# A two-stage attention and token-mixing kernel on one core: all operations in a new order

## The chip, the cores and the metric

The kernel runs on one core of a Trainium2 chip. The core has five engines that run side by side, each with its own queue of instructions taken in order: TensorE (PE: matmuls, with their weight loads shown apart as PEld), VectorE (DVE), ScalarE (ACT), GpSimd (POOL) and SyncE (SP, which here only requests transfers). Transfers between memory (DRAM) and on-chip memory (SBUF) are requested by an instruction in some engine's queue and run on 16 DMA engines. Matmul results go to PSUM, eight banks of 512 float32 columns over 128 partitions, and are brought to SBUF by VectorE or ScalarE ("evicted"). The metric is the device time of one execution in microseconds.

## The reference

Batch 8, 8 heads, 576 tokens, head size 64, 32 packed queries, model size 512, hyper size 64. All inputs and the output are float32.

```python
def sm_attn(qq, kk, vv):                      # per batch and head
    s = scale * np.matmul(qq, kk.transpose(0, 1, 3, 2))
    s = s - np.max(s, axis=-1, keepdims=True)
    a = np.exp(s)
    a = a / (np.sum(a, axis=-1, keepdims=True) + 1e-09)
    return np.matmul(a, vv)
p_packed = sm_attn(p, k, v)                   # 32 rows per head
out = sm_attn(q, p_packed, p_packed)          # 576 rows per head
...
x = out.transpose(0, 2, 1, 3).reshape(B, S, H * D)
wq = x @ w_q
wk = x @ w_k
W_tok = scale * np.einsum('bsd,btd->bst', wq, wk)
mixed = np.einsum('bst,btd->bsd', W_tok, x)
return np.maximum(mixed, 0.0) @ w_out
```

## The kernel before

The work is cut into some 650 small operations. Each is a Python function that issues one to some tens of instructions, and a long string, SCHEDULE, names them one after another: `kt1@2:3` is operation kt1 for batch 2 with PSUM bank 3, `ke1@2s` its eviction on ScalarE (`s`; `v` is VectorE, `g` GpSimd), and a letter `f` or `c` says whether a matmul takes all 128 weight columns at once or two halves. The loop at lines 827 to 833 walks through the string and calls the functions. Every engine gets its instructions in the order of the string, and the waits between engines are put in by the framework. So the string alone sets each engine's queue.

The operations for one batch, in the order of the data:

- LK, LQ, LV (line 149): loads of k, q and v, requested by GpSimd, converted to bfloat16 on the way. Batch 0's k comes differently: KA and KB (line 170) load its two halves as float32 (k_f) from SyncE's queue, and cA0, cA1, cB0, cB1 (line 251) cast them. PF (line 167) requests p of batch 0 (p_f) from ScalarE's queue, pfc (line 215) casts it to p_h, tp (line 220) transposes it, lp (line 227) scales it into pT_bd. PB (line 180) loads p of all batches; tr and lq (lines 234 and 242) do the same for batches 1 to 7. cw0 to cw3 (line 279) load w_q and w_k (wqk), wo0 and wo1 (line 288) w_out.
- kt0, kt1 (line 305): transposes of k, evicted by ke0, ke1 to kT; for batch 0 kf0 to kf3 (line 258) and kfe0 to kfe3. qt0, qt1, qe0, qe1: the same for q.
- s0 (line 346): scores of the packed queries. nm0 (line 356): their row maximum. ex0, ex1 (line 360): exponentials with row sums. rc1 (line 370), rm (line 409, GpSimd): reciprocal and a mask with it. xt0, xt1 (line 377), xe0, xe1: transposes of the exponentials. pv (line 422): times v. pp (line 431): normalised and masked. pt, pte: transposed (ppT).
- e0, e1 (line 471), e2 (line 484): scores of the 576 queries against the packed rows. For batches 0 to 3 mn0 to mn2 (line 532) take the negative maximum, ea0 to ea2 (line 540) add it on TensorE, xa0 to xa2 (line 546) exponentiate; for batches 4 to 7 mx, sb and x0 (lines 501, 505 and 556) do so with a subtraction on VectorE.
- sm0 (line 562, or on GpSimd lines 565 to 568): row sums. rr0 (line 572): reciprocals. ml0 to ml2 (line 576): normalised weights a, products of two tensors on VectorE or GpSimd.
- at0, at1 (lines 596 and 599), ae0, ae1: transposes of a. pq (line 450), pqe: packed rows times w_q and w_k. wk, wz, wq (lines 654, 665 and 686), g (709), y (725), m0, m1 (740), r (the relu), m2 (765), then o0 to o4 (line 782): the mixing and the projection, and st0 to st2 and sc (lines 816, 812 and 800) the stores, requested by SyncE.
- w1, w2 (line 204): filler matmuls on zeros, whose results are not used.

Nearly all evictions run through one helper, `evict`, so many rows of the profile carry its lines: 136 (ScalarE), 138, 140 and 142 (VectorE).

Buffers rotate by batch: six each for k, q and v. Requests of GpSimd stand in its queue between its arithmetic.

Of the kernel before, what the change touches and what calls it, by code (L numbers as in the profile page):

```python
# [7 lines left out]


SCHEDULE = """  # L10
    id@0 PB@0 w1@0c:1 LQ@0 w1@0c:0 w1@0c:0 w1@0c:5 PF@0 LV@0 w1@0c:7 w1@0c:1 KB@0 LK@1 w2@0c:2
    pfc@0s LK@2 w1@0c:1 cB0@0v KA@0 LQ@1 cB1@0v w1@0c:2 cA1@0s w1@0f:3 kf2@0:7 kfe2@0v w1@0c:3 cw1@0
    kf3@0:1 cA0@0v tp@0:7 lp@0s w1@0f:6 kf0@0:0 kfe3@0v cw0@0 cw2@0 kfe0@0v kf1@0:3 kfe1@0s tr@0:76
    lq1@0s cw3@0 s0@0:3 qt0@0:2 w1@0f:0 w1@0f:0 nm0@0 ex0@0 ex1@0 w1@0f:6 lq0@0s qt1@0:0 xt0@0c:4
    xt1@0f:3 w1@0f:5 rc1@0 qe1@0v w1@0f:0 LV@1 rm@0 xe0@0v w1@0f:7 xe1@0s pv@0:3 qe0@0v w1@0c:0 pp@0
    pt@0c:2 pte@0v e0@0c:4 kt1@1:1 ke1@1s mn0@0 e2@0:3 mn2@0 kt0@1:0 ke0@1v e1@0c:7 w1@0f:5 mn1@0
    LK@3 LQ@2 ea2@0c LV@2 s0@1:0 ea0@0c LK@4 xa2@0 ea1@0f xa0@0 w1@0c:5 nm0@1 xa1@0 sm0@0v wo1@0
    ex0@1 kt1@2:3 wo0@0 rr0@0 ml0@0v ex1@1 w1@0f:5 kt0@2:7 ke1@2s ke0@2s qt1@1:5 ml1@0v qe1@1v
    xt0@1c:1 qt0@1:2 xt1@1c:0 LV@3 xe1@1v rc1@1 rm@1 ml2@0v at0@0f:4 qe0@1s w1@0f:3 s0@2:5 at1@0f:3
    pq@0:2 xe0@1v ae0@0s pv@1:0 nm0@2 ae1@0s pqe@0s ex0@2 wk@0f:2 wz@0 pp@1 pt@1c:0 pte@1v LQ@3  # L20
    wq@0:1 wkx@0 ex1@2 e1@1f:0 e0@1f:5 mn0@1 e2@1:7 mn2@1 wke@0s g@0f:2 ge@0v wqe@0s xt1@2f:4
    xt0@2f:6 ea0@1c mn1@1 xe1@2s kt1@3:2 xe0@2v LK@5 xa0@1 ea2@1f xa2@1 ea1@1f xa1@1 ke1@3v pq@1:6
    rc1@2 y@0:4 ye@0v pqe@1s kt0@3:1 ke0@3s rm@2 w1@0f:2 m1@0:45 sm0@1v rr0@1 ml1@1g r11@0s qt1@2:2
    qe1@2s qt0@2:1 qe0@2v s0@3:5 pv@2:1 r10@0s ml0@1g nm0@3 m0@0:04 pp@2 pt@2f:1 r00@0v ex1@3
    at0@1f:2 pte@2v ml2@1g ex0@3 r01@0v LQ@4 at1@1f:3 e1@2f:1 e0@2f:0 ae0@1s LV@4 mn1@2 ae1@1s LK@6
    e2@2:6 mn2@2 kt0@4:7 kt1@4:4 ke1@4s LQ@5 ke0@4v mn0@2 wk@1f:3 wz@1 wke@1v wkx@1 wq@1:2 ea2@2c
    rc1@3 rm@3 xa2@2 ea1@2c xa1@2 pq@2:7 pqe@2s wqe@1v ea0@2c xa0@2 s0@4:3 xt0@3f:6 xe0@3s xt1@3f:1
    xe1@3s nm0@4 g@1f:2 sm0@2v rr0@2 o3@0f:7 LK@7 ml1@2g ge@1s ml2@2v ex1@4 ex0@4 rc1@4 o2@0f:0
    ml0@2g o0@0c:2 oe0@0v LV@5 oe3@0s y@1:3 pv@3:5 LV@6 pp@3 ye@1s xt0@4f:1 xe0@4v m1@1:34 r11@1v
    rm@4 oe2@0s m0@1:27 r00@1v qt0@3:0 qt1@3:5 r10@1s xt1@4c:4 r01@1s xe1@4s pt@3c:7 pte@3v LQ@6  # L30
    at1@2f:2 m2@1f:1 qe1@3v at0@2f:7 qe0@3s o1@0f:4 ae0@2s e1@3f:3 e0@3f:6 r2@1v kt1@5:0 ae1@2v
    pq@3:5 mn1@3 mn0@3 e2@3:2 mn2@3 oe1@0s pqe@3v ea1@3c kt0@5:7 LQ@7 ea0@3f ea2@3f ke1@5s xa1@3
    ke0@5v xa0@3 wk@2f:4 wz@2 qt1@4:0 wq@2:3 wke@2v wkx@2 qe1@4v s0@5:5 g@2f:4 xa2@3 sm0@3g wqe@2s
    qt0@4:0 ge@2s y@2:3 ye@2s nm0@5 ex0@5 ex1@5 qe0@4v pv@4:1 pp@4 o2@1c:3 rr0@3 m0@2:01 oe2@1s
    m1@2:24 r11@2s ml0@3g pt@4f:5 r10@2s r01@2s pte@4v o1@1f:6 e1@4f:5 e0@4f:4 r00@2v at0@3f:0
    ae0@3s oe1@1v mx0@4 xt0@5f:2 e2@4:6 xe0@5s kt0@6:1 pq@4:3 pqe@4s ke0@6s mx2@4 o0@1c:0 ml1@3g
    kt1@6:2 oe0@1s mx1@4 ml2@3g sb2@4 st0@1 qt1@5:6 xt1@5f:1 at1@3f:0 sb1@4 sb0@4 x0@4 ae1@3s ke1@6v
    s0@6:3 rc1@5 qe1@5v sm0@4g o4@1f:2 xe1@5s wk@3f:0 kt0@7:1 nm0@6 ex1@6 kt1@7:6 wz@3 rm@5 oe4@1v
    ke0@7v wkx@3 ke1@7v qt0@5:2 wq@3:1 ex0@6 rc1@6 wke@3s qe0@5s pv@5:3 s0@7:5 rr0@4 pp@5 xt0@6f:2
    pt@5f:3 ml0@4g wqe@3s nm0@7 xt1@6f:4 g@3f:0 LV@7 o3@1f:1 pte@5s e0@5f:3 ge@3v xe0@6s ml1@4g  # L40
    o2@2f:2 e1@5f:0 ex0@7 xe1@6v ml2@4g at1@4f:4 mx0@5 ex1@7 at0@4f:5 sb0@5 oe3@1s y@3:6 mx1@5
    e2@5:3 rm@6 st1@0 oe2@2s ye@3s ae0@4s xt0@7c:1 rc1@7 rm@7 mx2@5 sb1@5 sb2@5 ae1@4v xe0@7s
    o3@2c:2 pv@6:6 pp@6 x0@5 m0@3:51 m1@3:03 r00@3s wk@4f:4 pt@6f:6 r01@3v wq@4:7 pte@6v oe3@2v
    pq@5:1 wz@4 st1@2 r10@3s pqe@5v wke@4v qt1@6:5 qt0@6:2 sm0@5g r11@3s o0@3c:0 qe0@6v o1@3c:1
    qe1@6s e0@6c:2 wkx@4 g@4c:3 e1@6c:5 wqe@4s oe1@3s st0@0 oe0@3v rr0@5 xt1@7c:6 mx0@6 e2@6:7
    qt1@7:0 xe1@7s ge@4v st1@1 st2@1 ml0@5g mx1@6 sb1@6 o0@2c:4 qe1@7s at0@5c:6 m2@3c:3 mx2@6 sb2@6
    o1@2c:5 ml1@5g sb0@6 ae0@5s ml2@5g at1@5c:0 r2@3s pv@7:1 x0@6 oe0@2s y@4:6 ae1@5v pp@7 ye@4v
    qt0@7:3 oe1@2s sm0@6g st0@3 wq@5:0 pt@7c:4 wk@5c:1 pte@7s m0@4:62 m1@4:75 qe0@7v wqe@5s wz@5
    wkx@5 wke@5v e0@7c:4 mx0@7 o4@3c:3 pq@7:0 r10@4s o2@3c:1 r00@4s sb0@7 r01@4s e2@7:2 e1@7c:7
    pq@6:6 rr0@6 mx1@7 r11@4s g@5c:4 mx2@7 sb2@7 pqe@7s oe4@3s o2@4c:0 ge@5s oe2@3s pqe@6s y@5:3  # L50
    ye@5s o3@3c:1 sb1@7 m2@5c:2 ml0@6g at0@6c:7 x0@7 ae0@6v ml1@6g r2@5s ml2@6g o3@4c:4 at1@6c:3
    oe2@4s sm0@7v ae1@6s o0@4c:5 st0@2 oe0@4s m1@5:07 rr0@7 ml2@7g ml1@7v m0@5:63 r00@5v ml0@7g
    o1@4c:2 r10@5s oe1@4v wk@6c:0 r01@5s at1@7c:6 wz@6 ae1@7v at0@7c:3 ae0@7v wq@6:5 o4@5c:2 st2@3
    wk@7c:3 wq@7:6 st0@4 r11@5s oe3@4s oe3@3s wqe@6s wz@7 o1@5c:5 wke@6s wqe@7s wkx@6 st1@3 g@6c:0
    oe1@5s ge@6s wkx@7 wke@7v g@7c:6 ge@7s o3@5c:3 st1@4 y@6:5 y@7:0 o2@5c:4 ye@6s oe3@5s m0@6:56
    r00@6s ye@7v m1@6:30 o0@5c:7 m2@7c:1 oe4@5v m0@7:52 r10@6v oe2@5v r11@6s st2@5 m1@7:03 r01@6s
    o0@6c:6 o1@6c:4 r00@7v r10@7v o2@6c:5 oe0@5s st0@5 oe0@6s r11@7v o3@6c:0 st1@5 oe1@6s r2@7v
# [12 lines left out]
def kernel(  # L70
# [460 lines left out]
    def nmax2(i, b):  # L531
        nc.vector.tensor_reduce(
            units(i, tile("mn", [P, NU, 1], bf16, b)), S_[b]["e", i], axis=AX, op=MAX, negate=True)

# [329 lines left out]
```

## Time and profile before

| what | value |
|---|---|
| median of 3 runs | 118.99 us (118.69 to 119.18) |
| the profiled execution, its time | 119.33 us |
| the profiled execution, its span in the trace | 117.6 us |
| granted TensorE clock | 1.00 |
| loaded through GpSimd's queue | 14.49 MB, 73.4% of 16 DMA engines' time over the span |
| requested by SyncE (stores and the first k) | 10.62 MB, 23.6% |

The profile is of one execution. The span is what its instructions cover; its time, taken from outside, is 1.73 us longer. Busy times are sums over an engine's instructions, in which overlapping matmuls count once. "Idle before" in a row is the time that the engine stood still ahead of the instruction, and the name behind it is the work that ended that wait. Matmul ends are modelled, so starts are the firmer numbers on TensorE.

### The profile page before, as it was taken

What the parts mean: (1) busy time and instruction counts of PE and PEld (TensorE: products, weight loads), DVE (VectorE), ACT (ScalarE), POOL (GpSimd) and SP (SyncE); (2) the same over time, 40 slices, a digit from 0 to 9 for tenths busy, and PEclk for the clock granted to TensorE, in tenths of its full rate; (3) what the DMA queues carried; (4) which work ended last, traced back from release to release, by engine and by line L of the source; (5) the groups of instructions that cost most, each with busy time, mean ns of one, the idle gap of its engine ahead of it and who ended that gap; (6) DMA issues with size and microseconds to landing.
All of it is one profiled execution on the core that took longest, in us unless ns stands there. A gap on an engine that the chain in (4) does not pass through costs nothing.

```text
span 117.6 us, 4918 instructions
## 1 busy us (share of the span) xinstructions
PE 106.7 (91%) x2134; PEld 70.1 (60%) x2134; DVE 88.7 (75%) x174; ACT 88.8 (76%) x172; POOL 56.4 (48%) x83
## 2 busy tenths in 40 slices
...
GB/s 62 373 206 207 209 207 208 189 207 208 208 209 205 209 207 209 207 209 207 209 206 211 220 329 241 212 198 377 380 165 112 66 8 233 308 89 307 381 355 117
DMA packets 18069, 25.47 MB, mean 217 GB/s; under 512 B 2176, under 2 KB 14720, under 8 KB 18048
## 3 DMA queue, kind: packets, MB, share of 16 engines
q0 software_dynamic: 13920, 14.49, 73.4%
q1 hardware_dynamic: 3856, 10.62, 23.6%
q8 instruction: 16, 0.26, 0.8%
...
q14 instruction: 5, 0.04, 0.1%
...
## 4 chain that ended last, share of the span: by engine, by line
PE 59%; DMA 28%; ACT 3%; POOL 3%; issue 1%; DVE 1%; SPq 1%; POOLq 0%; ACTq 0%; DVEq 0%
PE psum L782 24%; DMA v_sb<-in_v_dram 20%; DMA out_dram<-o_sb 8%; PE psum L305 8%; PE psum L740 4%; PE psum L422 3%; PE psum L686 3%; PE psum L596 2%; PE psum L471 2%; PE psum L654 2%; PE psum L377 2%; PE psum L540 2%; PE psum L709 1%; ACT o_sb L136 1%; PE psum L438 1%
## 5 line engine op out<-in xcount | busy, mean ns | idle before, releaser
L782 PE MATMUL psum<-w_out,r 128*64 128x512 bf16 (+2 forms) x240 | 31.9, 373 | 0.5 <-ACT o_sb L136 0.5
L576 POOL TENSOR_TENSOR a<-e,rr 128x512 bf16<-128x512 f32 (+1 forms) x19 | 16.0, 866 | 9.1 <-DVE rr L572 4.1
L782 PEld LDWEIGHTS <-r 128*64 128x64 bf16 (+1 forms) x240 | 13.3, 109 | 11.0 <-issue 2.6
L136 ACT ACTIVATE o_sb<-psum 128x512 f32<-128x512 f32 (+1 forms) x25 | 14.4, 587 | 5.0 <-PE psum L782 4.2
L360 ACT ACTIVATE e1T<-psum,nmax 128x576 bf16<-128x576 f32 x16 | 11.7, 739 | 2.2 <-DVE nmax L356 2.2
L136 ACT ACTIVATE kT<-psum 128x1280 bf16<-128x1280 bf16 (+2 forms) x8 | 8.5, 1080 | 5.2 <-PE psum L305 4.9
L356 DVE TENSOR_REDUCE nmax<-psum 128x2 f32<-128x1152 f32 x8 | 10.8, 1355 | 2.1 <-PE psum L346 1.9
L305 PE MATMUL psum<-ident,q_sb 128*64 128x128 bf16 x288 | 10.4, 220 | 2.1 <-DMA q_sb<-in_q_dram 2.1
L136 ACT ACTIVATE r<-psum 128x512 bf16<-128x512 f32 x20 | 10.7, 610 | 0.8 <-PE psum L740 0.8
L204 PE MATMUL psum<-zero 128*64 128x512 bf16 (+1 forms) x39 | 9.8, 497 | 1.3 <-DVE zero L183 1.2
L305 PEld LDWEIGHTS <-q_sb 128*64 128x64 bf16 x288 | 8.5, 110 | 3.8 <-DMA q_sb<-in_q_dram 2.6
L565 POOL TENSOR_TENSOR rt<-e 128x576 f32<-128x576 f32 x4 | 5.7, 1416 | 8.6 <-ACT e L556 7.9
L305 PE MATMUL psum<-ident,k_sb 128*64 128x128 bf16 x252 | 9.1, 220 | 0.0
L149 POOL DMA_DIRECT2D v_sb<-in_v_dram x8 | 6.1, 767 | 5.7 <-DMA v_sb<-in_v_dram 2.9
L305 PEld LDWEIGHTS <-k_sb 128*64 128x64 bf16 x252 | 7.9, 110 | 1.0 <-issue 0.2
L138 DVE TENSOR_SCALAR r<-psum 128x512 bf16<-128x512 f32 x12 | 7.9, 683 | 0.6 <-PE psum L740 0.6
L149 POOL DMA_DIRECT2D q_sb<-in_q_dram x8 | 6.2, 779 | 4.6 <-PE psum L305 2.3
L142 DVE COPY qT<-psum 128x1280 bf16<-128x1280 bf16 (+1 forms) x10 | 7.5, 751 | 0.6 <-PE psum L305 0.4
L142 DVE COPY o_sb<-psum 128x512 f32<-128x512 f32 x8 | 5.5, 687 | 3.0 <-ACT o_sb L136 2.2
L136 ACT ACTIVATE e<-psum 128x512 bf16<-128x512 bf16 (+1 forms) x10 | 6.3, 639 | 1.1 <-PE psum L377 1.1
L149 POOL DMA_DIRECT2D k_sb<-in_k_dram x7 | 5.4, 770 | 3.6 <-DMA k_sb<-in_k_dram 3.0
L142 DVE COPY kT<-psum 128x1024 bf16<-128x1024 bf16 (+3 forms) x10 | 6.6, 662 | 0.6 <-PE psum L305 0.3
...
## 6 DMA issues: line engine op xcount, KB each, us to landing
...
```

The costliest lines, as they stand in the source:

```text
L136: nc.scalar.activation(dst, src, func, scale=scale)
L138: nc.vector.tensor_scalar(dst, src, 0.0, None, op0=MAX)
L142: nc.vector.tensor_copy(dst, src)
L149: nc.gpsimd.dma_start(t.rearrange("p g j d -> p g (j d)"), src[b].rearrange("(g h2) (sp j) d -> (h2 sp) g (j d)", h2=2, j=NJ),)
L204: nc.tensor.matmul(bank(ks[0])[r], zero[:, r], zero, start=True, stop=True, skip_group_check=True,)
L305: nc.tensor.transpose(tp[64 * g2:64 * g2 + 64, gp, :, 64 * (j - j0):64 * (j - j0) + 64], S_[b][src][:, gp + 2 * g2, order[j]], ident,)
L356: nc.vector.tensor_reduce(tile("nmax", [P, 2], fp32, b), S_[b]["s1"], axis=AX, op=MAX, negate=True)
L360: nc.scalar.activation(tile("e1T", [P, NJ, 2, 64], bf16, b)[:, :, h2], S_[b]["s1"][:, h2].rearrange("a (j s) -> a j s", j=NJ), EXP, bias=S ...
L565: nc.gpsimd.tensor_tensor(t, e[:, :, 0:16], e[:, :, 16:32], op=ADD)
L576: (nc.gpsimd if on == "g" else nc.vector).tensor_tensor(tile("a2", [P, NU, L], bf16, b)[:, r], S_[b]["e2"][:, r], S_[b]["rr"][:, r].to_bro ...
L740: nc.tensor.matmul(S_[b]["m", gp, h2], S_[b]["y"][r, 128 * gp:128 * gp + 128], S_[b]["wqT"][r, :], start=True, stop=True,)
L782: nc.tensor.matmul(ps[r, 0:w.stop - w.start], src[:, i, r], w_out[:, i, w], start=(i == 0), stop=(i == 3),)
```

## The change

The string is replaced by another with nearly the same operations. All of batch 0 to 7's operations are there once in both. Differences in kind: many evictions change between ScalarE and VectorE (operations on ScalarE in the string 116 before, 111 after; on VectorE 88 and 91; on GpSimd 23 and 25), some matmuls change between `f` and `c`, banks change, and four of the fillers w1 become two w2. In the first part of the string the order goes from

```
    id@0 PB@0 w1@0c:1 LQ@0 w1@0c:0 w1@0c:0 w1@0c:5 PF@0 LV@0 w1@0c:7 w1@0c:1 KB@0 LK@1 w2@0c:2
    pfc@0s LK@2 w1@0c:1 cB0@0v KA@0 LQ@1 cB1@0v w1@0c:2 cA1@0s w1@0f:3 kf2@0:7 kfe2@0v w1@0c:3 cw1@0
    kf3@0:1 cA0@0v tp@0:7 lp@0s w1@0f:6 kf0@0:0 kfe3@0v cw0@0 cw2@0 kfe0@0v kf1@0:3 kfe1@0s tr@0:76
    lq1@0s cw3@0 s0@0:3 qt0@0:2 w1@0f:0 w1@0f:0 nm0@0 ex0@0 ex1@0 w1@0f:6 lq0@0s qt1@0:0 xt0@0c:4
    xt1@0f:3 w1@0f:5 rc1@0 qe1@0v w1@0f:0 LV@1 rm@0 xe0@0v w1@0f:7 xe1@0s pv@0:3 qe0@0v w1@0c:0 pp@0
    pt@0c:2 pte@0v e0@0c:4 kt1@1:1 ke1@1s mn0@0 e2@0:3 mn2@0 kt0@1:0 ke0@1v e1@0c:7 w1@0f:5 mn1@0
    LK@3 LQ@2 ea2@0c LV@2 s0@1:0 ea0@0c LK@4 xa2@0 ea1@0f xa0@0 w1@0c:5 nm0@1 xa1@0 sm0@0v wo1@0
    ex0@1 kt1@2:3 wo0@0 rr0@0 ml0@0v ex1@1 w1@0f:5 kt0@2:7 ke1@2s ke0@2s qt1@1:5 ml1@0v qe1@1v
    xt0@1c:1 qt0@1:2 xt1@1c:0 LV@3 xe1@1v rc1@1 rm@1 ml2@0v at0@0f:4 qe0@1s w1@0f:3 s0@2:5 at1@0f:3
    pq@0:2 xe0@1v ae0@0s pv@1:0 nm0@2 ae1@0s pqe@0s ex0@2 wk@0f:2 wz@0 pp@1 pt@1c:0 pte@1v LQ@3
...
```

to

```
    id@0 PB@0 LQ@0 w1@0c:0 KA@0 cA1@0s cA0@0s LV@0 w1@0c:1 LK@1 KB@0 w2@0f:2 w2@0f:3 w1@0c:3 w1@0f:0
    w1@0c:6 LK@2 w1@0c:0 LQ@1 w1@0c:6 cB0@0s cB1@0v PF@0 kf0@0:3 w1@0f:6 LV@1 kf2@0:0 cw2@0 pfc@0v
    tp@0:6 lp@0v kfe2@0v kf1@0:4 cw3@0 kfe0@0s kfe1@0s kf3@0:1 kfe3@0v tr@0:53 s0@0:0 nm0@0 cw0@0
    lq0@0s cw1@0 w1@0c:4 qt0@0:6 ex0@0 ex1@0 rc1@0 qt1@0:4 qe0@0v w2@0f:7 xt1@0c:1 xt0@0f:0 w1@0c:7
    qe1@0s xe0@0s w1@0f:6 w1@0c:6 lq1@0s w1@0f:6 xe1@0v rm@0 pv@0:0 pp@0 pt@0f:5 w1@0c:1 w1@0c:7
    pte@0v e2@0:5 mn2@0 e0@0c:6 e1@0c:3 kt1@1:1 mn0@0 ea2@0c kt0@1:0 ke1@1s xa2@0 w1@0f:4 LK@3 LQ@2
    w1@0f:4 mn1@0 ea1@0c ke0@1v ea0@0c s0@1:0 xa1@0 xa0@0 kt1@2:3 ke1@2s nm0@1 ex1@1 ex0@1 kt0@2:6
    ke0@2v sm0@0v rr0@0 s0@2:3 LV@2 ml2@0g rc1@1 rm@1 qt1@1:6 qe1@1s LK@4 xt0@1f:0 xt1@1f:1 xe1@1s
    nm0@2 xe0@1v qt0@1:2 w1@0c:6 w1@0c:6 ex0@2 ex1@2 wo1@0 pv@1:0 ml0@0v ml1@0v pp@1 wo0@0 rc1@2
    pq@0:6 pqe@0v pt@1f:0 at0@0f:1 at1@0c:3 qe0@1s pte@1v e2@1:2 mn2@1 pq@1:0 e0@1f:6 ae0@0s e1@1f:1
...
```

The last two lines of both strings, with the last stores:

```
-   oe2@6v r01@7v st0@6 oe3@6s o4@7c:1 oe4@7s st1@6 st2@7 o3@7c:2 oe3@7s sc3@7 o0@7c:0 oe0@7v sc0@7
-   o1@7c:4 oe1@7s sc1@7 o2a@7c:0 o2b@7c:6 oe2a@7s sc2a@7 oe2b@7s w1@0f:7 sc2b@7
...
+   sc3@7 o4@7c:4 o0@7c:6 oe0@7s o2a@7c:2 oe1@7v sc1@7 oe4@7v st2@7 o2b@7c:7 sc0@7 oe2b@7v oe2a@7s
+   sc2a@7 w1@0f:6 sc2b@7
```

Beside the string, e2 may now be called without a bank (it then takes the second bank behind e0's), and maximum, shift and exponential get a form for all 36 score units at once:

```diff
-    def e2(b, ks):
-        S_[b]["e2bank"] = ks[0]
-        ps = bank(ks[0])[:, 0:128]
+    def e2(b, ks=None):
+        S_[b]["e2bank"] = ks[0] if ks else S_[b]["ebank", 0] + 2
+        ps = bank(S_[b]["e2bank"])[:, 0:128]
...
+    def whole(b):
+        S_[b]["e", 6] = bank(S_[b]["ebank", 0], fp32, 3)[:, 0:NU * L].rearrange("s (u l) -> s u l", l=L)
...
     def units(i, t):
+        if i == 6:
+            return t
...
-    for i in range(6):
+    for i in range(7):
...
+    def shifts(b, md):
+        for i in range(3):
+            shift(i, b, md)
+
+    ops["ea6"] = shifts
+    ops["mn6"] = lambda b: nmax2(6, b)
+    ops["xa6"] = lambda b: exps(6, b)
```

The new string names e2 with a bank each time, and none of the forms for all units.

87 lines of the change are left out of this document (40 added, 47 removed).

## The prediction

> **What bounds the kernel now.** I read the page first (span, busy shares, granted clock), then the busy time by stages with VectorE's and ScalarE's share, then filler matmuls alone, then the timeline of the first 30 us.
>
> ```profile
> span 117.6 us, 4918 instructions
> PE 106.7 (91%) x2134; PEld 70.1 (60%) x2134; DVE 88.7 (75%) x174; ACT 88.8 (76%) x172; POOL 56.4 (48%) x83
> ```
> ```profile
> 0.00:14.48 14.48, 11.62 (x158) 6.25 (x159) 8.20 (x21) 7.67 (x19) 7.80 (x16) 1.00 0.99 211
> 14.48:27.11 12.63, 10.13 (x244) 7.22 (x245) 9.97 (x18) 7.98 (x13) 6.43 (x10) 1.00 1.29 203
> 27.11:75.00 47.89, 46.43 (x988) 32.94 (x987) 44.09 (x85) 41.99 (x85) 29.00 (x40) 1.00 1.20 218
> 75.00:113.26 38.26, 38.26 (x747) 23.65 (x745) 26.48 (x52) 30.83 (x56) 13.13 (x18) 1.00 0.65 225
> 113.26:117.60 4.34, 0.31 (x1) 0.01 (x1) 0.00 (x0) 0.38 (x1) 0.00 (x0) 1.00 0.51 182
> ```
> ```profile
> 0.00:27.11 27.11, 9.06 (x37) 2.89 (x37) 1.00 1.13 208
> 27.11:117.60 90.49, 0.78 (x2) 0.19 (x2) 1.00 0.94 219
> ```
>
> The columns of the stage rows are the stretch, its length, the busy time of PE, PEld, DVE, ACT and POOL, the granted clock and the DMA share and GB/s; the last two rows are the same for the fillers (L204) alone, whose results nobody reads. From 75 us to 113.26 us TensorE has no gap at all (38.26 of 38.26). From 27.11 to 75 it loses 47.89 - 46.43 = 1.46 us of gaps, and fillers take some 0.39 of the 0.78 us behind 27.11 (one of two matmuls; the other lies in the tail), so 1.85 us. Before 27.11, 11.62 + 10.13 = 21.75 us are busy but 9.06 are fillers: 12.69 us of real work in 27.11 us, 14.4 lost. So the kernel is a head in which work waits for its inputs, then a TensorE-bound stretch, then a tail of 4.34 us (last eviction and last stores). A new order cannot shorten the TensorE stretch by more than its 1.85 us; what remains is the head and the tail. The head is therefore where I follow the change, step by step.
>
> ```profile
> 0.73 0.48 ACTq L167 DMA_DIRECT2D p_f<-in_p_dram  x1
> 5.12 1.02 DVE L142 CAST k_sb<-k_f 128x640 bf16<-128x640 f32 x2 [1.27 <-DMA k_f<-in_k_dram]
> 5.33 0.31 ACT L136 ACTIVATE p_h<-p_f 128x128 bf16<-128x128 f32 x1 [2.80 <-DMA p_f<-in_p_dram]
> 6.67 0.63 ACT L136 ACTIVATE k_sb<-k_f 128x512 bf16<-128x512 f32 x1 [1.02 <-DMA k_f<-in_k_dram]
> 6.73 0.22 PE L220 MATMUL psum<-ident,p_h 128*128 128x128 bf16 x1
> 8.01 1.08 PE L234 MATMUL psum<-ident,p_b 128*64 128x128 bf16 x32
> 8.93 0.66 PE L346 MATMUL psum<-kT,pT_bd 128*64 128x512 bf16 x8
> 9.71 1.36 DVE L356 TENSOR_REDUCE nmax<-psum 128x2 f32<-128x1152 f32 x1 [1.49 <-PE psum L346]
> 11.10 0.74 ACT L360 ACTIVATE e1T<-psum,nmax 128x576 bf16<-128x576 f32 x1 [0.77 <-DVE nmax L356]
> 12.46 0.20 ACT L360 ACTIVATION_READ_ACCUMULATOR e1T<-psum,nmax 128x1 f32 x1
> 14.48 0.70 PE L422 MATMUL psum<-v_sb,e 64*64 64x128 bf16 x36
> 14.62 0.75 POOL L149 DMA_DIRECT2D v_sb<-in_v_dram  x1 [2.88 <-DMA v_sb<-in_v_dram]
> 16.05 0.42 DVE L431 TENSOR_TENSOR pp<-psum,rm 128x256 bf16<-128x256 f32 x1 [1.22 <-POOL rm L409]
> 17.22 0.44 PE L471 MATMUL psum<-ppT,qT 128*64 128x64 bf16 x16 [0.39 <-DVE ppT L142]
> 19.54 0.68 PE L346 MATMUL psum<-kT,pT_bd 128*64 128x512 bf16 x8
> 26.15 0.40 PE L596 MATMUL psum<-ident,a 128*128 128x128 bf16 x4
> 26.38 0.28 PE L599 MATMUL psum<-ident,a 128*128 128x128 bf16 x2
> 26.59 0.30 PE L450 MATMUL psum<-wqk,ppT 128*64 128x128 bf16 x4
> 27.11 0.70 PE L422 MATMUL psum<-v_sb,e 64*64 64x128 bf16 x36 [0.22 <-DMA v_sb<-in_v_dram]
> ```
>
> Each row is start, duration, engine, line, operation, and in brackets how long the engine stood idle and for what. The milestones of batch 0 are s0 at 8.93, pv at 14.48, e0 at 17.22; of batch 1, s0 at 19.54 and pv at 27.11, the last waiting for its v load. That load is the last thing that holds TensorE for want of data.
>
> **The change part by part.** The work is the same; engines swap some evictions, four single fillers become two double ones, and the added functions (whole, shifts, mn6, xa6, ea6) have no name in the new order, so they issue nothing. What moves on the path is this.
>
> **1. The request for p_f.** Before it is the first thing in ScalarE's queue (0.73). Now ScalarE's queue holds cA1, cA0 and cB0, the casts of the first k, ahead of it, and cB0 waits for the second half of k_f. I keep the two arrivals of before, 5.12 and 6.67, with the halves' names swapped as on SyncE's queue. cA1 takes 0.63 (the row at 6.67); a cast of 640 columns I put at 0.75, between 0.705 (first row below, the same width from PSUM) and 0.63 x 640/512 = 0.79. The other rows are for the steps behind.
>
> ```profile
> L136 ACT ACTIVATE e<-psum 128x640 bf16<-128x640 bf16 x4 | 2.8, 705 | 0.0
> L136 ACT ACTIVATE qT<-psum 128x1280 bf16<-128x1280 bf16 x3 | 3.7, 1239 | 0.3 <-PE psum L305 0.2
> L136 ACT ACTIVATE pT_bd<-psum 64x128 bf16<-64x128 bf16 x2 | 0.5, 263 | 0.0
> L142 DVE COPY kT<-psum 128x640 bf16<-128x640 bf16 x2 | 1.0, 492 | 0.3 <-PE psum L258 0.2
> L142 DVE COPY kT<-psum 128x1024 bf16<-128x1024 bf16 x4 | 2.8, 692 | 0.3 <-PE psum L305 0.3
> L532 DVE TENSOR_REDUCE mn<-psum 128x16 bf16<-128x512 f32 x8 | 5.4, 684 | 1.0 <-PE psum L471 1.0
> L562 DVE TENSOR_REDUCE rs<-e 128x36 f32<-128x1152 f32 x4 | 5.4, 1343 | 0.0
> ```
>
> 5.12 + 0.63 + 0.75 = 6.50, cB0 starts at 6.67 and ends at 7.42: p_f is requested 6.7 us later than before.
>
> **2. Its landing, F.**
>
> ```profile
> out_dram<-o_sb SPq DMA_DIRECT2D x2, 128.0 KB, 2.1
> p_f<-in_p_dram ACTq DMA_DIRECT2D x1, 64.0 KB, 4.6
> wqk<-in_moe_w_q_dram POOLq DMA_DIRECT2D x2, 32.0 KB, 17.5
> ```
>
> The columns are the issuing queue, the count, the size of each, and the time from request to landing. The same p_f request took 4.6 us when the k halves ran beside it; the quickest transfer of the trace, 128 KB, took 2.1. So F lies between 7.42 + 2.1 = 9.5 and 7.42 + 4.6 = 12.0. The k halves are gone by then but the POOL loads run on (DMA share 0.99), so I take the middle, 10.7. The Trainium skill (DMA: Bandwidth & Descriptors, Anatomy of one DMA — SWDGE (gpsimd) path) fits a transfer as about 2.0 us fixed plus bytes over 436 GB/s, an estimate of 2.15 us here, though for the POOL path; by it F would be 9.6 and the sum 1.1 us smaller. The row of 4.6 disagrees with that fit.
>
> **3. F to s0 of batch 0.** On VectorE and TensorE in order: the p_h cast 0.31, tp 0.22, then lp in two halves of 0.26, kfe2 0.49, kfe3 about 0.42, with handovers 2.2. TensorE's own part (tp, kf1, kf3, and tr, which takes 8.93 - 8.01 = 0.92) is shorter. Before, this step took 3.6 from 5.33, as it waited for the second half of k. s0 starts at 12.9 instead of 8.93.
>
> **4. s0 to pv of batch 0.** The exponentials end 12.66 - 8.93 = 3.73 after s0 starts. Then ScalarE now has qe1 (1.24) ahead of xe0 (0.70), which pv needs: 3.73 + 1.24 + 0.70 + 0.05 = 5.7 (before: 5.55). pv at 18.6; its v has been there since 14.6 at the latest (GpSimd's wait in that row).
>
> **5. pv to e2, the first scores.** Before 2.74, of which pp waited 1.22 for GpSimd's rm, held by the load at 14.62. The four small wqk loads now take that waiting, and rm is ready early. pv 0.75, then pp to scores as before, 17.22 - 16.05 = 1.17: 1.9; the two fillers between pt and e2 put it at 2.3 if they are in the way. I take 2.15: e2 at 20.75.
>
> **6. e2 to s0 of batch 1.** Before e0 to s0 took 2.32. Now e2, e0 and e1 all go ahead of kt1, and VectorE has three maxima (0.28 by size, 0.68, 0.68) ahead of ke0 (0.69). 0.45 until e2 can be read, the chain of these four 2.35, and the wait for e0's end 0.3: 3.1. s0 of batch 1 at 23.85 instead of 19.54.
>
> **7. s0 to pv of batch 1.** Before 7.57, set by data. Now data is there. s0 and its maximum take 0.78 + 1.36 = 2.15; ke1 of batch 2 (1.24) is ahead of the exponentials on ScalarE, which end at about 4.25; VectorE goes nm0 2.15, ke0 of batch 2 0.69, the row sum 1.34, two reciprocals 0.5, a second maximum 1.36, then xe0 0.49: 6.5. pv at +6.6, at 30.45. That is 3.35 later than 27.11; with F at its ends, 2.15 and 4.65.
>
> **8. What is left at that point.** In the old order at0, at1 and pq of batch 0 stood ahead of pv of batch 1, now they stand behind it: 0.23 (as 26.15 to 26.38) for at0, 0.44 for at1 (26.15 to 26.59), 0.23 for pq: 0.9 us more for TensorE to do.
>
> **9. The middle.** The 1.85 us lost there can be won, no more; the other end I take as 1.5 of new gaps, as evictions have moved to a VectorE already busy 44.09 of 47.89. Later stores touch one stall here, and room for GpSimd is worth little:
>
> ```profile
> 73.48 0.60 ACT L136 ACTIVATE o_sb<-psum 128x512 f32<-128x512 f32 x1 [0.72 <-DMA out_dram<-o_sb]
> L576 POOL TENSOR_TENSOR a<-e,rr x19: 394/1046/1078, 34.9 to 95.7; 128x512 bf16<-128x512 f32 x13, 128x128 bf16<-128x128 f32 x6
> ```
>
> GpSimd's slowest product is 1078 ns against a median of 1046, so there is little stretching to remove: at most 13 x 0.03 = 0.4 us, on an engine 48% busy. I take -0.6 for the whole middle, the store's stall of 0.72 with hardly more.
>
> **10. The tail.** Same last projection; the last shared store (st2 of batch 7) now stands among the final single stores instead of ahead of them: +0.2 (0 to 0.5).
>
> Sum: 3.35 + 0.9 - 0.6 + 0.2 = 3.9 (3.85). The profiled execution took 119.33, 0.34 above the median of 118.99; so 123.2 for it, and 122.9 against the median.
>
> **The rivals.** *The clock falls.* TensorE finishes kf2 at about 7.9 and, with one matmul tp waiting for p_f and everything queued behind, stands still until F + 0.4 = 11.1: 3.2 us. Before, its longest idle time in the stages shown was 14.48 - 11.62 = 2.86 in all, in pieces, and the clock was 1.00 in every row. If TensorE then runs at half speed (assumed), kf1, kf3, tr and s0, some 2.1 us of TensorE, take twice that, of which about 1.5 is on the path: 124.4. Against it: the wait is near the edge. The Trainium skill (TensorE: Matmul & The Clock Gate, Part 1) says that an idle window of about 3.4 us halves the clock, in a free-running window; no row here shows it.
>
> *The lateness is absorbed, and it is faster.* Batch 1's v is requested ahead of the wqk loads, so it lands some 0.6 earlier (four loads of 32 KB, two for q as in the row and two like them for k, at the 203 to 211 GB/s of the first two stages), and pv could start at 26.5. This decides only if F + 19.75 is at most 26.5, F no later than 6.75, which is before the second half of k allows the request at all; so it needs my steps to be 3 us too long. Then -0.6 + 0.9 - 1.3 for the middle = -1.0: 118.0.
>
> *Nothing is seen.* F at 9.5 takes 1.2 off, a middle without any gap 1.25 more; if step 7 then runs 1.4 shorter, the sum is 0: 119.0.
>
> **How the numbers follow.** Forecast (122.9) 0.65; clock 0.18; nothing seen 0.08; absorbed 0.09. The forecast's own range is 120.4 (3.85 - 1.2 - 1.25) to 124.9 (one of +1.3 and +2.1 whole). I reach to 119.7 and 125.6 for the rivals. A change of less than 0.5% can't be told from none here. Faster: absorbed and a quarter of nothing seen, 0.11. Same: half of it, 0.04; slower 0.85.
>
> **What would show it.** p_f requested near 7.4 on ScalarE's queue; the p_h cast, now on VectorE, between 9.5 and 12; s0, pv, e2, s0, pv at about 12.9, 18.6, 20.7, 23.8, 30.4; clock 1.00 throughout; from there on TensorE full. I am wrong if p_f is requested early, if pv of batch 1 starts by 28, or if the gaps come after 40 us.

## The result and the profile after

The changed kernel takes 125.31 us (median of 4 executions, 125.24 to 125.47) against 119.09 us for the kernel before in the same comparison (median of 4, 118.69 to 119.54): a ratio of 1.0525, 95% interval 1.0482 to 1.0567. It is 6.2 us slower; the forecast was 3.9 us slower (122.9 us). The profiled execution took 125.47 us, 6.14 more than that of before.

First the page of the changed kernel: its span, TensorE's busy tenths and granted clock in 40 slices of 3.1 us, and the chain of work that ended last.

```profile
span 123.7 us, 4922 instructions
...
PE   6930697796989989999999999999999999999960
...
PEclk9998559999999999999999999999999999999999
...
PE psum L798 26%; PE psum L305 9%; DMA p_f<-in_p_dram 5%; DMA k_f<-in_k_dram 4%; PE psum L377 3%; PE psum L471 3%; PE psum L612 3%; PE psum L756 3%; DVE nmax L356 3%; PE psum L702 3%; PE psum L346 3%; PE psum L422 3%; PE psum L670 2%; PE psum L549 2%; PE psum L204 2%; ACT qT L136 2%
```

One slice (the fourth, 9.3 to 12.4 us) has no matmul at all, in the next two the clock is down to half, and the transfer of p_f alone is 5% of the chain of waits: 6 us. From the seventh slice on the clock is full. The stages, cut as before (length, busy time of PE, PEld, DVE, ACT, POOL, granted clock, DMA share, GB/s):

```profile
0.00:14.48 14.48, 7.02 (x57) 2.85 (x59) 4.00 (x15) 4.12 (x6) 8.36 (x17) 0.90 0.99 210
14.48:27.11 12.63, 11.32 (x225) 7.88 (x222) 5.98 (x12) 7.25 (x17) 2.86 (x4) 0.84 1.29 203
27.11:75.00 47.89, 45.41 (x1014) 32.92 (x1015) 43.59 (x78) 42.45 (x84) 28.07 (x39) 1.00 1.20 203
75.00:113.26 38.26, 38.26 (x799) 24.27 (x793) 33.23 (x70) 31.30 (x60) 17.81 (x26) 1.00 0.55 194
113.26:123.70 10.44, 6.29 (x65) 3.44 (x61) 3.84 (x6) 1.47 (x3) 0.00 (x0) 1.00 0.66 258
```

TensorE is busy 7.02 us of the first 14.48, where it was 11.62 before. The second stage looks fuller than before (11.32 against 10.13), but at a clock of 0.84: part of that is the same work taking longer. The last row holds what the loss pushed behind 113.26: 6 us of matmuls and then the tail. The head in the timeline shows where the 6 us arose:

```profile
6.25 0.74 ACT L136 ACTIVATE k_sb<-k_f 128x640 bf16<-128x640 f32 x1 [0.30 <-DMA k_f<-in_k_dram]
6.26 0.42 ACTq L167 DMA_DIRECT2D p_f<-in_p_dram  x1
7.04 0.47 PE L258 MATMUL psum<-ident,k_sb 128*64 128x128 bf16 x10 [0.25 <-ACT k_sb L136]
13.05 0.23 DVE L142 CAST p_h<-p_f 128x128 bf16<-128x128 f32 x1 [6.17 <-DMA p_f<-in_p_dram]
13.33 0.29 PE L220 MATMUL psum<-ident,p_h 128*128 128x128 bf16 x1 [5.82 <-DVE p_h L142]
14.41 1.92 PE L234 MATMUL psum<-ident,p_b 128*64 128x128 bf16 x32
16.11 1.17 PE L346 MATMUL psum<-kT,pT_bd 128*64 128x512 bf16 x8
...
33.25 0.70 PE L422 MATMUL psum<-v_sb,e 64*64 64x128 bf16 x36 [0.15 <-DVE e L142]
...
116.53 1.46 SPq L816 DMA_DIRECT2D out_dram<-o_sb  x2
...
119.16 0.39 PE L204 MATMUL psum<-zero 128*128 128x512 bf16 x1
```

p_f is requested at 6.26 and its cast starts at 13.05, 6.8 us later. The cast waits for nothing but that transfer (6.17 us of idle time on VectorE), and behind it tp stands still on TensorE for 5.82 us. pv of batch 1, the milestone at which the prediction ends its head, starts at 33.25 instead of 27.11: 6.14 us later. The last filler, behind the last projection, starts at 119.16 instead of 113.18, where the kernel before has it:

```profile
113.18 0.39 PE L204 MATMUL psum<-zero 128*128 128x512 bf16 x1
```

That is 5.98 later. So the whole loss is there by pv of batch 1, and nothing is added or won back behind it beyond 0.2 us. TensorE's clock around the wait (busy time, clock, DMA share, GB/s):

```profile
10.00:15.00 5.00, 1.67 (x29) 0.66 1.21 204
15.00:20.00 5.00, 4.65 (x74) 0.66 1.21 208
```

The clock falls inside the wait, at a time when TensorE does nothing anyway, and stays low for the first 5 us of work behind it: tr takes 1.92 us where it took 1.08 before, s0 1.17 where it took 0.66.

### The profile page after: what moved, and what is told of

Same layout as the page of the kernel before. It is cut to its first block, busy times and chain, and to the rows that moved or that the text cites. A ratio compares the mean times of both kernels' runs of the same rounds, so it can differ in the third digit from the quotient of the medians.

```text
span 123.7 us, 4922 instructions
## 1 busy us (share of the span) xinstructions
PE 108.3 (88%) x2136; PEld 71.4 (58%) x2136; DVE 90.6 (73%) x178; ACT 86.6 (70%) x166; POOL 57.1 (46%) x85
## 4 chain that ended last, share of the span: by engine, by line
PE 74%; DMA 9%; DVE 8%; ACT 4%; issue 1%; SPq 0%; DVEq 0%
PE psum L798 26%; PE psum L305 9%; DMA p_f<-in_p_dram 5%; DMA k_f<-in_k_dram 4%; PE psum L377 3%; PE psum L471 3%; PE psum L612 3%; PE psum L756 3%; DVE nmax L356 3%; PE psum L702 3%; PE psum L346 3%; PE psum L422 3%; PE psum L670 2%; PE psum L549 2%; PE psum L204 2%; ACT qT L136 2%
## 5 line engine op out<-in xcount | busy, mean ns | idle before, releaser
L592 POOL TENSOR_TENSOR a<-e,rr 128x512 bf16<-128x512 f32 (+1 forms) x21 | 17.0, 831 | 21.3 <-DVE rrec L370 12.4
L136 ACT ACTIVATE o_sb<-psum 128x512 f32<-128x512 f32 (+1 forms) x18 | 10.2, 587 | 5.6 <-PE psum L798 5.5
L360 ACT ACTIVATE e1T<-psum,nmax 128x576 bf16<-128x576 f32 x16 | 11.7, 736 | 3.1 <-DVE nmax L356 3.1
L136 ACT ACTIVATE kT<-psum 128x1280 bf16<-128x1280 bf16 (+3 forms) x6 | 6.0, 1006 | 9.7 <-PE psum L258 6.7
L142 DVE COPY o_sb<-psum 128x512 f32<-128x512 f32 (+1 forms) x15 | 10.0, 667 | 3.8 <-PE psum L798 3.8
L136 ACT ACTIVATE qT<-psum 128x1280 bf16<-128x1280 bf16 (+1 forms) x9 | 10.3, 1144 | 0.0
L136 ACT ACTIVATE e<-psum 128x640 bf16<-128x640 bf16 (+1 forms) x11 | 7.1, 654 | 2.0 <-PE psum L377 2.0
L409 POOL TENSOR_TENSOR rm<-mask,rrec 128x256 f32<-128x256 f32 x8 | 5.0, 628 | 7.3 <-DVE rrec L370 7.3
L142 DVE COPY kT<-psum 128x1024 bf16<-128x1024 bf16 (+3 forms) x12 | 8.1, 691 | 0.2
L508 DVE TENSOR_REDUCE mx<-psum 128x16 f32<-128x512 f32 (+1 forms) x12 | 6.4, 551 | 1.4 <-ACT o_sb L136 1.2
L377 PE MATMUL psum<-ident,e1T 128*128 128x128 bf16 (+1 forms) x89 | 6.4, 220 | 0.8 <-ACT e1T L360 0.7
L541 DVE TENSOR_REDUCE mn<-psum 128x16 bf16<-128x512 f32 (+1 forms) x12 | 6.2, 551 | 1.1 <-ACT a2T L136 0.5
```

The lines of the kernel that those rows point to most:

```text
L136: nc.scalar.activation(dst, src, func, scale=scale)
L142: nc.vector.tensor_copy(dst, src)
L360: nc.scalar.activation(tile("e1T", [P, NJ, 2, 64], bf16, b)[:, :, h2], S_[b]["s1"][:, h2].rearrange("a (j s) -> a j s", j=NJ), EXP, bias=S ...
L377: nc.tensor.transpose(tp[r, j - j0, :], S_[b]["e1T"][:, j].rearrange("a h s -> a (h s)")[:, r], ident,)
L541: nc.vector.tensor_reduce(units(i, tile("mn", [P, NU, 1], bf16, b)), S_[b]["e", i], axis=AX, op=MAX, negate=True)
L592: (nc.gpsimd if on == "g" else nc.vector).tensor_tensor(tile("a2", [P, NU, L], bf16, b)[:, r], S_[b]["e2"][:, r], S_[b]["rr"][:, r].to_bro ...
```

## The experiments

Two questions are open. Is the place of p_f's request the cause, or one of the other changes in the order that I cannot separate in one trace? And why does a transfer of 64 KB, which took 4.6 us before, take 6.8? After these comes the price of the clock, and a last part looks for an order that beats both kernels. All ratios are against the kernel before on the same chip; "later" and "earlier" are against the changed kernel unless said.

### The request's place: e1_pf_first and e2_before_pf_late

The first is the changed kernel with one name moved:

```diff
-    id@0 PB@0 LQ@0 w1@0c:0 KA@0 ...
+    PF@0 id@0 PB@0 LQ@0 w1@0c:0 KA@0 ...
...
-    ... cB0@0s cB1@0v PF@0 kf0@0:3 ...
+    ... cB0@0s cB1@0v kf0@0:3 ...
```

> The changed order with PF alone moved to the head of the string, so that ScalarE requests p_f ahead of the casts, as before the change. Theory (the late p_f is the whole loss): p_f is requested at about 0.7 and lands by 5.5, s0 of batch 0 starts at 9 to 10, pv of batch 1 at 27 to 28, the clock is 1.00 throughout, and the time is 118.2 to 119.8 us. Rival (the rest of the new order is slower as well): p_f lands as early, but the time stays above 121 us.

119.07 us, ratio 1.0016 (0.9992 to 1.0040). Of the 6.2 us at most 0.5 is left. Its timeline, and its row of requests (size and time to landing):

```profile
0.75 0.47 ACTq L167 DMA_DIRECT2D p_f<-in_p_dram  x1
...
7.43 0.21 DVE L142 CAST p_h<-p_f 128x128 bf16<-128x128 f32 x1
...
26.50 0.70 PE L422 MATMUL psum<-v_sb,e 64*64 64x128 bf16 x36 [0.15 <-DVE e L142]
```
```profile
p_f<-in_p_dram ACTq DMA_DIRECT2D x1, 64.0 KB, 4.7
```

p_f lands at 0.75 + 4.7 = 5.4. The cast of p_h has no idle time ahead of it: here it waits in VectorE's queue behind the k cast there (cB1, at 6.83), not for p_f. pv of batch 1 follows at 26.50. That is 0.6 earlier than in the trace of the kernel before, and the span is 0.7 shorter (116.9 against 117.6); but the profiled execution of the kernel before took 119.33 us, 0.4 above the median in this comparison (118.90), and by the medians nothing is left of it. The second is the counterpart, the kernel before with p_f's request moved back:

```diff
-    ... w1@0c:5 PF@0 LV@0 ...
-    pfc@0s LK@2 w1@0c:1 cB0@0v KA@0 LQ@1 cB1@0v w1@0c:2 cA1@0s w1@0f:3 kf2@0:7 ...
+    ... w1@0c:5 LV@0 ...
+    LK@2 w1@0c:1 cB0@0v KA@0 LQ@1 cB1@0v w1@0c:2 cA1@0s PF@0 pfc@0s w1@0f:3 kf2@0:7 ...
```

> The old order with PF and pfc alone moved behind cA1 in ScalarE's queue. Theory: p_f is requested at about 6.7, lands at about 13.5 (6.8 us beside GpSimd's loads, as in the changed kernel), TensorE stands still for some 5 us, s0 of batch 0 starts near 16.5 instead of 8.93, and the time is 123.5 to 125.5 us. Rival (the late p_f costs this much only together with the new order's longer steps): below 122 us.

125.29 us, ratio 1.0526 (1.0501 to 1.0552): as slow as the changed kernel, with everything else in the old order.

```profile
6.16 0.42 ACTq L167 DMA_DIRECT2D p_f<-in_p_dram  x1
12.96 0.31 ACT L136 ACTIVATE p_h<-p_f 128x128 bf16<-128x128 f32 x1 [6.19 <-DMA p_f<-in_p_dram]
...
33.85 0.70 PE L422 MATMUL psum<-v_sb,e 64*64 64x128 bf16 x36
```

Again 6.8 us from request to cast (the cast itself, pfc, stands behind the request on ScalarE, as the edit has it). The two runs together settle the first question: the one moved request makes the loss, and the rest of the new order is worth nothing that can be told here (0.2 us, with an interval that holds 0).

### Why the transfer is slow: e4_pf_sp, e5_pf_alone, e9_pf_rows

Here p_f is requested by SyncE, behind the halves of k, so that it doesn't wait for casts:

```diff
-    ... LK@1 KB@0 w2@0f:2 ...
-    ... cB1@0v PF@0 kf0@0:3 ...
+    ... LK@1 KB@0 PF@0 w2@0f:2 ...
+    ... cB1@0v kf0@0:3 ...
...
-        nc.scalar.dma_start(p_f, ...)
+        nc.sync.dma_start(p_f, ...)
```

> The changed order with p_f requested by SyncE behind the two halves of k, and not by ScalarE. Theory: requested at about 1.7, it lands by 7.5, the first half of k lands near 4.7 as in the changed kernel, and the time is within 0.5 us of the run with PF first, 118.2 to 119.8 us. Rival (p_f's landing is slow whenever GpSimd's loads run beside it): it lands after 8.5 us and the time is above 120 us.

120.40 us, ratio 1.0119 (1.0074 to 1.0165). The rival held:

```profile
1.75 0.47 SPq L167 DMA_DIRECT2D p_f<-in_p_dram  x1
...
7.00 0.47 PE L258 MATMUL psum<-ident,k_sb 128*64 128x128 bf16 x10 [0.16 <-ACT k_sb L136]
8.80 0.23 DVE L142 CAST p_h<-p_f 128x128 bf16<-128x128 f32 x1 [1.91 <-DMA p_f<-in_p_dram]
```

The request went out at 1.75, and the cast still started 7.05 us later. The transfer is slow with another issuing queue and at another time too, with GpSimd's loads beside it (its requests for q, v and k follow from 2.17 us on). This run alone doesn't name those loads as the cause, since the two halves of k stand ahead of p_f in SyncE's queue here, and the casts of the second half start only at 6.21. So the next kernel holds these loads back until p_f has landed, by a small product on GpSimd that reads p_f (PW, a result that nobody uses):

```diff
-    id@0 PB@0 LQ@0 w1@0c:0 KA@0 cA1@0s cA0@0s LV@0 w1@0c:1 LK@1 KB@0 ...
-    w1@0c:6 LK@2 w1@0c:0 LQ@1 w1@0c:6 cB0@0s cB1@0v PF@0 kf0@0:3 ...
+    id@0 PB@0 w1@0c:0 KA@0 cA1@0s cA0@0s w1@0c:1 KB@0 ...
+    w1@0c:6 w1@0c:0 w1@0c:6 cB0@0s cB1@0v PF@0 PW@0 LQ@0 LV@0 LK@1 LK@2 LQ@1 kf0@0:3 ...
```

> The changed order with GpSimd's loads of q, v and k (five of them, from q of batch 0 on) held back until p_f has landed, by a small product on GpSimd that reads p_f; p_f is requested where the changed order has it, at about 6.2 us. Theory (GpSimd's loads beside it are what make p_f slow): it lands 2.1 to 3.8 us after its request, against 6.8 in the changed kernel. Rival (the request is slow by itself, for its 256 pieces of 256 bytes): 5.5 us or more. The time itself is of no use here, as all loads come later: 124 to 128 us.

```profile
6.31 0.42 ACTq L167 DMA_DIRECT2D p_f<-in_p_dram  x1
8.15 0.23 DVE L142 CAST p_h<-p_f 128x128 bf16<-128x128 f32 x1 [1.42 <-DMA p_f<-in_p_dram]
```

Requested at the same time and by the same queue as in the changed kernel, p_f is there 1.84 us later instead of 6.8. The halves of k are there before the request in both kernels, so GpSimd's loads are what differs; the landing is even quicker than the 2.1 to 3.8 us of the theory. The time, 122.99 us in a single execution, missed its expectation (124 to 128) on the low side: q of batch 0 is requested at 8.58 instead of 2.16, and that cost less than I had put. In the third, p_f comes in rows of 2 KB (it changes the computation: batch 0's p lies in other places, and only a quarter of each row is used):

```diff
-        nc.scalar.dma_start(p_f, p[0].rearrange("(g x) l d -> (x l) g d", g=2))
+        nc.scalar.dma_start(p_f2, p[0].rearrange("h (a c) d -> (h a) (c d)", c=8))
```

> The changed order, but p_f is brought as 32 rows of 2 KB in place of 256 pieces of 256 bytes, at the same place in ScalarE's queue; the values of batch 0's p then stand in other places, and only the first quarter of each row is used. Theory (each piece waits its turn among the pieces of the loads, so the wait goes with their number): landing 2.5 to 4.5 us after the request, and the time 120.5 to 123 us. Rival (the transfer as a whole waits behind the loads, whatever its pieces): 6 us or more and 124.5 to 125.5 us.

124.13 us, ratio 1.0445 (1.0421 to 1.0469). From the page of this kernel the row of the queue that carries p_f (packets, MB, share), and from its timeline the request and the cast:

```profile
q10 hardware_dynamic: 48, 0.07, 0.2%
```
```profile
6.14 0.38 ACTq L168 DMA_DIRECT2D p_f<-in_p_dram  x1
...
11.45 0.21 DVE L142 CAST p_h<-p_f 32x128 bf16<-32x128 f32 x1 [4.50 <-DMA p_f<-in_p_dram]
```

The same queue's row of the changed kernel has 272 packets. 224 packets fewer carry the same bytes, and the cast starts 5.3 us behind the request instead of 6.8: between the two expectations, as is the time. So larger pieces (on 32 partitions instead of 128, which isn't told apart from their size) take off some 1.5 us; what sets the other 3.5 us above the 1.84 of e5 these runs leave open.

### What the clock costs: e3_fill, e6_fill_again, e10_fill15, e7_after_again, e11_fill_moved

If TensorE is given filler matmuls while it waits for p_f, the clock should stay up and the time show what the low clock costs. The edit in the changed kernel, 22 fillers or 15:

```diff
-    ... kf2@0:0 cw2@0 pfc@0v
+    ... kf2@0:0 cw2@0 w22@0f:7 pfc@0v
```

> The changed order with 22 more filler matmuls (some 4.8 us at full clock) between kf2 and tp, into a bank that nobody uses then, while TensorE waits for p_f. Theory (the lower clock made the steps behind p_f longer): granted clock 1.00 from 10 to 20 us, s0 of batch 0 about 2.2 us behind the p_h cast instead of 3.06, time 123.8 to 124.6 us. Rival (the steps are bound by VectorE and ScalarE, and the clock does not matter): the clock is kept, the time stays within 0.4 us of 125.3.

The clock was 1.00 in the first two stages, s0 of batch 0 came 1.8 us behind the cast of p_h instead of 3.06 and pv of batch 1 at 31.45, 1.8 us earlier; and the time was 125.12 us, ratio 1.0525 (1.0465 to 1.0586): nothing won. The rival's time held, but not its reason, as the steps did get shorter. Three more kernels follow: the same one again, the changed kernel itself for comparison, and one with fewer fillers.

> The changed order with 22 more fillers in the wait for p_f once more, with more rounds, beside the changed kernel on the same chip. Theory (the lower clock cost time in the head, 1.8 us at pv of batch 1 in the first look): 0.8 us or more below the changed kernel. Rival (what the head gains is lost again behind it): within 0.4 us of the changed kernel.

> The changed kernel itself, for the comparison with the run with fillers on one chip. Both theories: 125.0 to 125.6 us, clock 0.97.

> The changed order with 15 instead of 22 fillers in the wait for p_f, so that the instruction fetches stay at the changed kernel's 16 packets (17 with 22 fillers). Theory (the clock costs 1.2 us up to the last matmul, and the longer tail of the runs with 22 fillers belongs to their extra instructions): clock 1.00, last matmul ends 1.0 to 1.4 us earlier than in the changed kernel, tail 4.4 us, time 123.9 to 124.4 us. Rival (the tail grows whenever the last stores come earlier): time within 0.4 us of 125.3.

They took 125.69 us (ratio 1.0575, 1.0552 to 1.0598), 125.30 us (1.0529, 1.0508 to 1.0550) and 125.58 us (1.0562, 1.0513 to 1.0610). With fillers, pv of batch 1 stands 1.6 to 1.8 us earlier in each trace, and nothing of it is in any of the times. The end of the run with 15 fillers:

```profile
115.41 2.21 SPq L816 DMA_DIRECT2D out_dram<-o_sb  x2
...
118.05 0.39 PE L204 MATMUL psum<-zero 128*128 128x512 bf16 x1
```

The last matmul is 1.11 us earlier than the changed kernel's 119.16, but the span is 123.7 as well: SyncE's two store requests take 2.21 us instead of 1.46, and the stretch from the last filler to the end is 5.65 us instead of 4.54. With 22 fillers the same stretch is 5.05 us (e3) and 5.6 (e6). These three fetch 17 packets of instructions, all other kernels 16; with 15 fillers I had expected 16. So it may be the extra instructions, not the clock, that take the gain back. The last kernel of this part keeps the number of instructions: all nine fillers before the first k transpose go (two of them double, and some in two halves: 17 matmuls), and 17 stand in p_f's wait.

```diff
-    id@0 PB@0 LQ@0 w1@0c:0 KA@0 cA1@0s cA0@0s LV@0 w1@0c:1 LK@1 KB@0 w2@0f:2 w2@0f:3 w1@0c:3 w1@0f:0
-    w1@0c:6 LK@2 w1@0c:0 LQ@1 w1@0c:6 cB0@0s cB1@0v PF@0 kf0@0:3 w1@0f:6 LV@1 kf2@0:0 cw2@0 pfc@0v
+    id@0 PB@0 LQ@0 KA@0 cA1@0s cA0@0s LV@0 LK@1 KB@0
+    LK@2 LQ@1 cB0@0s cB1@0v PF@0 kf0@0:3 w1@0f:6 LV@1 kf2@0:0 cw2@0 w17@0f:7 pfc@0v
```

> The changed kernel with fillers moved: the single fillers before kf0 are taken out and 17 single fillers stand between kf2 and tp of batch 0, where TensorE stood idle for 5.8 us. The number of instructions is then about that of the changed kernel, which it was not in the two runs with added fillers. Question: what the lower clock of the head costs in time. Theory (the clock costs about 1 us of the 6.2): the clock is low only at the very start and 1.00 from about 12 us, s0 of batch 0 starts about 1.8 us behind the p_h cast instead of 3.06, pv of batch 1 at about 31.5 instead of 33.25, the last matmul ends at about 118.0 instead of 119.24, the tail is 4.4, and the time is 123.9 to 124.4. Rival (what the head wins is lost again): the head is as early, but the last matmul or the tail comes later, and the time lies within 0.4 of 125.3.

123.66 us, ratio 1.0400 (1.0387 to 1.0414): 1.65 us below the changed kernel by the medians, 1.5 by the ratios, a little more than the theory's range.

```profile
6.02 0.74 PE L258 MATMUL psum<-ident,k_sb 128*64 128x128 bf16 x10 [6.02 <-ACT k_sb L136]
...
13.08 0.23 DVE L142 CAST p_h<-p_f 128x128 bf16<-128x128 f32 x1 [6.19 <-DMA p_f<-in_p_dram]
...
15.12 0.70 PE L346 MATMUL psum<-kT,pT_bd 128*64 128x512 bf16 x7
...
31.84 0.70 PE L422 MATMUL psum<-v_sb,e 64*64 64x128 bf16 x36 [0.15 <-DVE e L142]
...
118.20 0.39 PE L204 MATMUL psum<-zero 128*128 128x512 bf16 x1
```

p_f is as late as before (13.08), s0 is 2.04 us behind it instead of 3.06, pv of batch 1 1.41 us earlier, the last filler 0.96, and the tail is not stretched (span 122.7, so 4.50 us). The profiled execution was the slowest of its six (124.49 us), so its trace shows only 1.0 us of gain at the end; by the median, the price of the clock is 1.5 to 1.65 us of the 6.2. That the extra instructions of the three other runs took their gain fits all four, and is not shown by itself: these kernels differ in the fillers at the start too. A second measure comes from two other kernels, whose executions differ in their mean clock. e4 took 119.89 and 119.98 us at 0.993 and above, 120.82 and 120.90 at 0.986 and below; e8, below, took 120.43 and 120.48 at 0.996 and above, 121.76 to 122.01 at 0.980 to 0.986. The lower clock goes with 0.8 to 1.6 us there.

### An order that beats both: e8_before_v1_first, e12_before_v1_rm

The kernel before, with what spoke for the rival of an absorbed loss: batch 1's v requested earlier, and pq of batch 0 behind pv of batch 1.

```diff
-    pfc@0s LK@2 w1@0c:1 cB0@0v KA@0 LQ@1 cB1@0v ...
+    pfc@0s LK@2 w1@0c:1 cB0@0v KA@0 LQ@1 LV@1 cB1@0v ...
...
-    ... w1@0f:0 LV@1 rm@0 ...
+    ... w1@0f:0 rm@0 ...
...
-    pq@0:2 xe0@1v ae0@0s pv@1:0 nm0@2 ...
+    xe0@1v ae0@0s pv@1:0 pq@0:2 nm0@2 ...
```

> The old order with one idea of the new one: v of batch 1 is requested ahead of the four small wqk loads, and pq of batch 0, which needs them, stands behind pv of batch 1. Theory (the head's last wait for data is that v load, 0.6 us earlier without the small loads ahead): pv of batch 1 at 26.4 to 26.8 instead of 27.11, the time 0.3 to 0.7 us below the kernel before. Rival (pv is then held by xe0, or the gain is lost behind it): within 0.2 us of the kernel before.

121.78 us, ratio 1.0200 (1.0143 to 1.0257): slower by 1.4 to 2.6%, which neither side had expected.

```profile
25.80 0.74 POOL L149 DMA_DIRECT2D k_sb<-in_k_dram  x1 [1.84 <-DMA v_sb<-in_v_dram]
26.48 0.70 PE L422 MATMUL psum<-v_sb,e 64*64 64x128 bf16 x36
26.53 1.24 POOL L288 DMA_DIRECT2D w_out<-in_moe_w_out_dram  x2
27.74 0.78 POOL L149 DMA_DIRECT2D v_sb<-in_v_dram  x1
28.50 0.65 POOL L409 TENSOR_TENSOR rm<-mask,rrec 128x256 f32<-128x256 f32 x1
...
29.19 0.42 DVE L431 TENSOR_TENSOR pp<-psum,rm 128x256 bf16<-128x256 f32 x1 [1.56 <-POOL rm L409]
```
```profile
30.00:35.00 5.00, 5.00 (x76) 3.38 (x72) 3.35 (x8) 2.57 (x6) 0.62 (x1) 0.69 1.21 208
```

pv is 0.63 us earlier, as meant, but rm of batch 1 stands behind four requests on GpSimd, the first of which waited 1.84 us, and pp waits 1.56 us for rm. The gain at one milestone was lost at the next. The last row (busy times, clock, DMA) shows a second loss: TensorE waited for pp in its turn, and its clock fell, to 0.69 from 30 to 35 us. The executions with a mean clock of 0.996 and above took 120.43 and 120.48 us, so some 1.6 us of the loss is the wait, and the rest goes with the clock. With rm ahead of those requests (LK@4, wo1 and wo0 leave their earlier places):

```diff
-    xt0@1c:1 ... LV@3 xe1@1v rc1@1 rm@1 ml2@0v ...
+    xt0@1c:1 ... xe1@1v rc1@1 rm@1 LK@4 wo1@0 wo0@0 LV@3 ml2@0v ...
```

> The kernel before with batch 1's v requested earlier and pq of batch 0 behind pv of batch 1, as in e8_before_v1_first, and now also with rm of batch 1 ahead of the loads LK4, wo1, wo0 and LV3 in GpSimd's queue, so that rm does not wait behind them. Theory (e8 was slower because rm of batch 1 came 1.5 us late behind those loads): pv of batch 1 starts at about 26.5, rm ends by 27.2, pp of batch 1 starts at about 27.2 instead of 29.2, the clock stays 1.00, and the time is 118.2 to 118.7, 0.2 to 0.7 below the kernel before. Rival (the loads that are now requested later hold something else): the time is 118.9 or more.

```profile
26.18 0.70 PE L422 MATMUL psum<-v_sb,e 64*64 64x128 bf16 x36
...
27.20 0.41 DVE L431 TENSOR_TENSOR pp<-psum,rm 128x256 bf16<-128x256 f32 x1
```

118.88 us, ratio 1.0002 (0.9991 to 1.0012). The order of e8 is explained, since its loss is gone with the wait for rm, and the milestones are where the theory has them or earlier (pv at 26.18, forecast 26.5); but no time is won over the kernel before, which is 118.90 us in the same comparison: the rival's time. As with e1, the trace of the kernel before is of one of its slower executions, so milestones set against it flatter. I have no version that beats the kernel before.

## Why the prediction was right, and where its sizes were off

The direction and the mechanism held: p_f's request behind the k casts makes batch 0 late, nothing absorbs it, and the whole loss stands at pv of batch 1. The size, 3.9 us against 6.2, was off mainly in one term. The result lies above the forecast's own range (120.4 to 124.9) and inside the one widened for the rivals (up to 125.6), which is partly luck: that range had no landing later than 12.0 in it, and it holds 125.3 because the price of a lower clock had been put on top. Of the signs named, two failed: the cast between 9.5 and 12 (13.05), and the clock at 1.00 throughout.

- **Step 1, the request.** Forecast 7.42, measured 6.26. It goes out 0.01 us after the cast ahead of it has started, not when it ends (0.74 us); and that cast started at 6.25, 0.42 earlier than the 6.67 taken over from before.
- **Step 2, the landing: the mis-sized term.** Forecast 10.7 (9.5 to 12.0), measured 13.05. The error is larger than it looks, as step 1 gave 1.16 us back: the transfer took 6.8 us where I had allowed 3.3, and at most 4.6. The low end came from a store of 128 KB (2.1 us) and the high end from p_f itself before GpSimd's loads were all in flight; the row of 17.5 us for 32 KB, which I had quoted, is also a small load beside the large ones (though behind them in GpSimd's own queue), and was not used as a bound. e5 shows the cause: 1.84 us without those loads. The Trainium skill (DMA: Bandwidth & Descriptors, Anatomy of one DMA — SWDGE (gpsimd) path) gave 2.15 us as an estimate for this transfer; that is near the 1.84 us measured without the loads and far from the 6.8 beside them, where the measurement decides.
- **Steps 3 to 7.** Forecast 19.75 us from the landing to pv of batch 1, measured 20.2 (33.25 - 13.05). That agreement is two errors: with the clock up it is 18.76 in e11 (31.84 - 13.08) and 19.07 in e1 from the cast on (26.50 - 7.43), so my steps were 0.7 to 1.0 us too long, and the low clock added 1.1 to 1.4.
- **The clock.** This was a rival at 0.18, and it came true together with the forecast, as its condition, a TensorE wait near 3 us, became 5.82 us through step 2. Its price was put at about 1.5 us; e11 gives 1.5 to 1.65 by the medians and 1.0 in its trace. The Trainium skill (TensorE: Matmul & The Clock Gate, Part 1) has an idle window of about 3.4 us halve the clock; the wait of 5.82 us agrees. In e4 it fell with less, as told below.
- **Steps 8 and 9, the work left and the middle.** Forecast +0.9 - 0.6 = +0.3; measured -0.16 (last filler 5.98 later, pv of batch 1 6.14 later). The stretch from pv of batch 1 to the last filler, before and after:

```profile
27.11:113.18 86.07, 84.61 (x1733) 56.52 (x1732) 70.57 (x137) 72.77 (x140) 42.12 (x58) 1.00 0.96 221
33.25:119.16 85.91, 84.66 (x1758) 57.05 (x1759) 74.91 (x144) 69.32 (x135) 44.30 (x62) 1.00 0.88 205
```

Gaps and fillers took 1.46 + 0.39 = 1.85 us before and 85.91 - 84.66 = 1.25 after (no filler falls into it): -0.6, as forecast. By these rows TensorE's own work grew by 84.66 - (84.61 - 0.39) = 0.44 us, not by 0.9. So the term that was off here is the work moved behind pv.
- **Step 10, the tail.** Forecast +0.2, measured +0.1 (4.54 against 4.42 us behind the start of the last filler).
- **Sum.** 3.35 at pv of batch 1 by the forecast, + 2.35 for the landing + 0.45 for steps 3 to 7 = 6.15 there (measured 6.14); - 0.16 + 0.12 behind it gives 6.1, the growth of the span from 117.6 to 123.7.
- **The absorbed loss.** The point from which it was to decide, F by 6.75, is met in e1: p_f lands at 5.4, and pv of batch 1 starts at 26.50, as forecast for that rival. Yet the time is that of before, not 1 us below it. e12 says the same from the other kernel: with pv of batch 1 at 26.18 its time is that of before too. (That rival also put the middle at -1.3, where the sum had -0.6 and -0.6 was measured.)

So, by the medians, about 4.6 of the 6.2 us is p_f's lateness itself (e11's 4.8 less the 0.2 of e1), and 1.5 to 1.65 the clock that fell while TensorE waited.
